# Attention units of one batch and four heads, with the second transposition moved from TensorE to the DMA queue of SyncE

## The chip, the cores and the metric

The kernel runs on one core of a Trainium2 chip. The metric is the device time of one execution in microseconds (us), as the median of several runs. A core has five engines with an instruction queue each: PE (TensorE: matmuls, which write to PSUM), DVE (VectorE), ACT (ScalarE), POOL (GpSimd) and SP (SyncE, which here only issues DMAs). Each engine works through its own queue strictly in order. [...]

## The reference

For 8 batches, 8 heads, 576 positions and a head size of 64, linear attention with a feature map of 128 + 128 features; then, on the eight heads side by side (512 features), a gated unit with a causal convolution of 5 taps:

```python
proj = q_or_k @ w_phi                              # 64 -> 128
proj = proj - max(abs(proj))                       # per position
phi = concat([exp(proj), exp(-proj)])              # 256 features
kv, z = phi(k).T @ v, sum(phi(k))                  # per head
x = (phi(q) @ kv) / (phi(q) @ z + 1e-6)
x = heads side by side                             # (8, 576, 512)
gate = sigmoid(sum over 5 taps of conv_w[tap] * x[position - 4 + tap])
out = (gate * (x @ w_val)) @ w_out
```

## The kernel before, in words

**Units and steps.** The attention is cut into 16 units. A unit of the kernel before is a pair of batches and a pair of heads (four units make a pair of batches); its Q, K and V are loaded for two units at a time by POOL, which casts them to bf16 on the way, into tiles of 128 partitions by 2 heads by 9 columns of 64 features. Two batches lie in the two partition halves of Q (`q_load`), while K and V are laid in four pieces (`kv_load`), so that eight of the nine columns hold one batch in all 128 partitions. Every unit takes three steps (`NG`), and `step(t)` writes the instructions of step t for all stages at once: K and Q of unit t // 3, the feature-major second projection three steps later (`LAGC`), the division seven steps later (`LAGN`). 48 steps carry units; the last steps only drain.

**The stages of a step**, by the letters of `ORDER`, which is the order in which their instructions enter the queues:

- K, k, x: PE projects K (`PK`), DVE takes the largest magnitude (`MK`), ACT writes the two exponentials (`KTIL`).
- T, t: PE transposes the K and Q of the next step (`T`), DVE copies them out (`QKT`).
- Q, q: PE projects Q (`PA`), DVE takes its maxima (`MQ`).
- C, c: PE projects Q once more in feature-major form (`PQ`), ACT writes the exponentials (`QTIL`).
- V, v (every third step): PE sums phi(k).T v (`KV`), DVE copies it (`KVSB`). V was scaled before on POOL (`VT`, two instructions of a unit).
- N, n: PE forms numerator and denominator (`NUM`), DVE divides (`RCP`, `XN`).
- X (three steps of twelve): PE transposes XN to feature-major form (`XP`), DVE copies that to `XT`, and POOL copies two shifted stretches of it for the taps (`emit_virt`).
- L, a, d: a list `mlp` of items of the gated unit. Each step adds `BUDGET[g]` to a purse and takes items as long as the purse is positive. An item is `emit_VG` (taps `GATE`, and `VAL`, on PE; then tanh `GS` on ACT and the product `GV` on DVE) or `emit_O` (output matmuls `OP`, copied by ACT to `OS`, stored by two DMAs of SP). What is left in the list after the last step is written behind it.

**PSUM.** `PK`, `PA`, `PQ`, `KV` and `GATE` take turns in three buffers of two banks, `T`, `NUM`, `XP`, `VAL` and `OP` in two buffers of one bank.

**A pair of batches as an amount of work for the gated unit:** four items with taps of 512 columns and two VAL results of 4 matmuls each, one small item (columns of chunk 8), and nine `OP`. They enter the list when both batches have all heads transposed: for the first pair at step 20, and for the last one behind step 55.

```python
BLOCKS = [[(ALL, b, c)] for b in range(2) for c in (0, 4, 1, 5)]
ORDER = "KkTtNVxQLnaCvXqdc"
LAGC, LAGV, LAGN, LAGM = 3, 4, 7, 1
BUDGET = (30, 30, 5)
```

## Time and profile before

| | |
|---|---|
| median of 3 runs | 270.02 us (269.23 to 270.37) |
| the profiled execution | 271.08 us |
| its span, first to last instruction | 269.3 us |
| PE busy | 227.3 us, 84% of the span |
| DVE busy | 192.3 us, 71% |
| ACT busy | 184.2 us, 68% |
| POOL busy | 142.3 us, 53% |
| mean granted TensorE clock | 0.949 of full speed |

A row of a timeline gives the start in us, the length in us, the engine, line, operation, output and inputs, and the number of instructions merged; in brackets stands how long the engine sat idle before and for whom it waited. Matmuls are pipelined, so the length of one overlaps the next; what a group costs PE is the distance from its start to the start of the next group. Shares over the whole span mix stages with different limits.

### The profile page before, as it was taken

The page shows a single profiled execution, that of the slowest core. Times are in us where ns is not written, and L with a number is a line of the kernel's source. Part 1 is how long each engine was busy: PE and PEld are TensorE (multiplying, and loading weights), DVE is VectorE, ACT ScalarE, POOL GpSimd, SP SyncE. Part 2 cuts the span into 40 slices and gives each one's busy share as a digit, 9 for nine tenths or more (in the row PEclk, how much of TensorE's full clock was granted, in tenths as well). Part 3 has the DMA queues.
Part 4 walks back from the last instruction along what each step waited for, and adds up shares of the span by engine and source line. Part 5 has one row for each costly group of instructions (what it writes and reads, how often), then busy time and mean ns, then how long its engine had stood idle before and what let it go on. Part 6 is the DMA issues. An engine that isn't in the chain of part 4 may idle for free.

```text
span 269.3 us, 8205 instructions
## 1 busy us (share of the span) xinstructions
PE 227.3 (84%) x3508; PEld 144.2 (54%) x3528; DVE 192.3 (71%) x342; ACT 184.2 (68%) x285; POOL 142.3 (53%) x190
## 2 busy tenths in 40 slices
PE   8578876676799988998799979987899899779992
PEld 4345665564656464666546455665555456533441
DVE  2597799999888497779878587888978553634221
ACT  1479799899576886988657777987569767111551
POOL 8979989999923945098416942336306060030000
PEclk9755799999999999999999999999999999977999
DMA  5999998925920894449800992520001505300536
GB/s 162 151 182 172 151 176 119 178 33 64 174 30 2 137 218 69 104 78 162 124 2 22 152 225 32 115 64 19 0 4 41 117 4 121 80 0 0 121 86 146
DMA packets 28948, 25.83 MB, mean 96 GB/s; under 512 B 2667, under 2 KB 24043, under 8 KB 28912
## 3 DMA queue, kind: packets, MB, share of 16 engines
q0 software_dynamic: 22128, 14.63, 39.5%
q1 hardware_dynamic: 6272, 10.06, 15.4%
q10 hardware_dynamic: 512, 0.62, 0.8%
q8 instruction: 27, 0.44, 0.7%
q14 instruction: 9, 0.07, 0.1%
HBM read 30.48 MB, written 9.44 MB: 148 GB/s over the span
## 4 chain that ended last, share of the span: by engine, by line
PE 48%; DVE 27%; ACT 18%; issue 3%; DMA 2%; ACTq 1%; POOL 0%; POOLq 0%; DVEq 0%
PE OP L471 12%; DVE MK L291 9%; PE VAL L463 9%; PE GATE L442 9%; ACT KTIL L296 9%; ACT QTIL L341 6%; DVE MQ L306 5%; DVE QKT L277 4%; PE KV L354 3%; PE NUM L376 3%; DVE XN L387 3%; PE XP L406 2%; PE PQ L329 2%; DVE GV L452 2%; ACT GS L448 2%
## 5 line engine op out<-in xcount | busy, mean ns | idle before, releaser
L317 POOL TENSOR_TENSOR VT<-VN,E 128x1152 bf16<-128x1152 bf16 x32 | 68.5, 2141 | 70.4 <-issue 61.7
L341 ACT ACTIVATE QTIL<-PQ 128x768 bf16<-128x768 f32 x96 | 73.2, 826 | 17.7 <-PE PQ L334 17.7
L296 ACT ACTIVATE KTIL<-PK 128x768 bf16<-128x768 f32 x96 | 73.1, 822 | 16.6 <-DVE MK L291 16.4
L452 DVE SCALAR_TENSOR_TENSOR GV<-GS,VAL 128x512 bf16<-128x512 bf16 (+1 forms) x40 | 24.8, 634 | 40.3 <-ACT GS L448 33.9
L291 DVE TENSOR_REDUCE MK<-PK 128x6 f32<-128x768 f32 x48 | 45.9, 956 | 9.6 <-PE PK L283 9.1
L306 DVE TENSOR_REDUCE MQ<-PA 128x6 bf16<-128x768 f32 x48 | 45.7, 951 | 0.0
L471 PE MATMUL OP<-WOUT,GV 128*128 128x512 bf16 x124 | 33.8, 379 | 4.9 <-DVE QKT L277 3.3
L448 ACT ACTIVATE GS<-GATE 128x1024 bf16<-128x1024 f32 (+1 forms) x20 | 18.8, 940 | 26.4 <-PE GATE L442 26.0
L463 PE MATMUL VAL<-XT,WVAL 128*128 128x512 bf16 (+1 forms) x192 | 36.4, 337 | 0.0
L476 ACT ACTIVATE OS<-OP 128x512 f32<-128x512 f32 x36 | 21.8, 607 | 13.3 <-PE OP L471 11.2
L376 PE MATMUL NUM<-KVSB,QTIL 128*128 128x65 bf16 (+1 forms) x640 | 29.9, 196 | 0.5 <-DVE XT L416 0.3
L283 PEld LDWEIGHTS <-QKT 64*128 64x128 bf16 x576 | 19.9, 98 | 18.6 <-issue 12.5
L277 DVE COPY QKT<-T 128x768 bf16<-128x768 bf16 (+2 forms) x49 | 27.6, 563 | 2.6 <-PE T L264 2.2
L387 DVE TENSOR_TENSOR XN<-NUM,RCP 128x384 bf16<-128x384 f32 x48 | 26.8, 558 | 1.6
L283 PE MATMUL PK<-W,QKT 64*128 64x128 bf16 x288 | 17.4, 229 | 12.1 <-ACT KTIL L296 9.6
L442 PE MATMUL GATE<-XT,DIAG 64*64 64x512 bf16 (+1 forms) x480 | 24.7, 338 | 2.0 <-POOL XT L423 1.2
L376 PEld LDWEIGHTS <-QTIL 128*128 128x128 bf16 (+1 forms) x640 | 24.6, 100 | 3.2 <-issue 0.7
L463 PEld LDWEIGHTS <-WVAL 128*128 128x128 bf16 x192 | 15.1, 100 | 19.6 <-issue 8.6
L264 PE MATMUL T<-ident_bf,QN 128*128 128x128 bf16 x144 | 23.3, 233 | 1.5 <-ACT QN L152 1.5
L264 PE MATMUL T<-ident_bf,KN 128*128 128x128 bf16 x144 | 23.7, 235 | 0.2 <-DVE KN L154 0.2
L471 PEld LDWEIGHTS <-GV 128*128 128x128 bf16 x144 | 13.0, 97 | 18.8 <-issue 4.0
L423 POOL COPY XT<-XT 128x504 bf16<-128x504 bf16 x16 | 9.3, 618 | 23.8 <-DVE XT L416 23.8
(50 smaller groups left out, 309.1 us busy)
## 6 DMA issues: line engine op xcount, KB each, us to landing
out_dram<-OS SPq DMA_DIRECT2D x72, 128.0 KB, 2.4
QN<-in_q_dram POOLq DMA_DIRECT2D x14, 288.0 KB, 7.5
VN<-in_v_dram POOLq DMA_DIRECT2D x16, 160.0 KB, 8.2
KN<-in_k_dram POOLq DMA_DIRECT2D x14, 160.0 KB, 5.3
VN<-in_v_dram POOLq DMA_DIRECT2D x16, 128.0 KB, 8.1
KN<-in_k_dram POOLq DMA_DIRECT2D x14, 128.0 KB, 4.4
WNAT<-in_moe_w_val_dram POOLq DMA_DIRECT2D x1, 512.0 KB, 7.5
WOUT<-in_moe_w_out_dram POOLq DMA_DIRECT2D x4, 128.0 KB, 7.2
```

Of the source, the lines that this page charges most:

```text
L264: nc.tensor.transpose(T[:, s * GC + i, :], src.rearrange("p h c d -> p (h c d)")[:, m * P:(m + 1) * P], ident_bf[:, :])
L277: nc.vector.tensor_copy(QKT[:, xs, :], T[:, xs, :])
L283: nc.tensor.matmul(PA[:, r, i * P:(i + 1) * P], u.T[g][half(r), s, i, :], W2[half(r), :], start=True, stop=True)
L291: nc.vector.tensor_reduce(u.MK[:, :].rearrange("p (m r) -> p r m", r=2)[:, :, blocks(g)], u.PK, AX.X, ALU.max, apply_absolute_value=True)
L296: nc.scalar.activation(u.KTIL[:, sg].rearrange("p (m r) f -> p r m f", r=2)[:, :, blocks(g), :], u.PK, AF.Exp, scale=1.0 - 2.0 * sg)
L306: nc.vector.tensor_reduce(mq, u.PA, AX.X, ALU.max, apply_absolute_value=True, negate=True)
L317: nc.gpsimd.tensor_tensor(VT[:, :, 0:D], u.VN.rearrange("p h c d -> p (h c) d"), eb.to_broadcast([P, 2 * NC, D]), ALU.mult)
L341: nc.scalar.activation(u.QTIL[:, sg, :, :, g * GC * D:(g + 1) * GC * D], PQ[:, :, 0:GT].rearrange("p r (b x) -> p r b x", b=2), AF.Exp, sc ...
L376: nc.tensor.matmul(NUM[ps, i, h, :], u.QTIL[:, sg, r, b, m * D:m * D + ps.stop - ps.start], u.KVSB[:, b, 2 * h + sg, :], start=(sg == 0), ...
L442: nc.tensor.matmul(GATE[half(c), r, z * n:(z + 1) * n], DIAG[half(r), jt, tap, :], cols(jt, 4 - tap, half(r)), start=(tap == 0), stop=(tap ...
L463: nc.tensor.matmul(VL[:, z, :], WVAL[:, dt, v * P:(v + 1) * P], cols(dt, 0), start=(dt == 0), stop=(dt == 3))
L471: nc.tensor.matmul(OP[:, :], pr.GV[g][:, jt // 2, jt % 2, i * P:(i + 1) * P], WOUT[:, jt, :], start=(jt == 0), stop=(jt == 3))
```

## The change

A unit is now one batch and four heads: heads 2hp and 2hp + 1 in the lower partition half, heads 4 + 2hp and 5 + 2hp in the upper one. K and V are loaded as Q is, by two DMAs each, where K and V took four. Every column of KTIL now holds two heads, so `pe_KV` works on partition halves throughout: 72 matmuls of 64 rows, where there were 32 of 128 rows and 8 of 64. A batch is finished every six steps, where a pair was finished every twelve.

XN is transposed into XT by DMA transposes that SP issues right behind the division of a batch's second unit (`dma_x`), ten for each of the first seven batches: eight of 128 positions by 256 features and two of 64 by 256. Only the last batch keeps the way by PE (`x_tile`), with one of its copies on ACT. POOL's shifted copies of a batch are written two steps behind its last transpose, and its items enter the list three steps behind it (`LAGX`).

The items of the gated unit are cut finer (taps, and each VAL result, apart) and are made per batch with 256 columns, the small item and its `OP` per pair. The budget is 8, 20 and 20 over the three steps of a unit, with the purse set to 0 while the list is empty. The letters of `ORDER` are rearranged: MQ's projection goes ahead of NUM, the products and the transposes last. At the start, 12 matmuls on zeros stand where there were 20, ACT and not POOL builds `EB`, and three loads fewer lead K and Q in. POOL's late constants move from steps 12 and 13 to 9 and 10.

```diff
-BLOCKS = [[(ALL, b, c)] for b in range(2) for c in (0, 4, 1, 5)]
+
+BLOCKS = [[(ALL, s, c)] for s, c in ((0, 0), (0, 4), (1, 0), (1, 4), (1, 1), (1, 5), (0, 1), (0, 5))]
 BLOCKS.insert(4, [(LO, 0, 8), (HI, 1, 8)])
+NB = len(BLOCKS)
...
-ORDER = "KkTtNVxQLnaCvXqdc"
+ORDER = "KTVkQtNxvnLCqadcX"
 LAGC, LAGV, LAGN, LAGM = 3, 4, 7, 1
-XACT = ()
-BUDGET = (30, 30, 5)
+LAGX = 3
+XACT = (8,)
+BUDGET = (8, 20, 20)
...
+    def load(T, x, u, nh, engs):
+        for s in range(2):
+            h0 = 4 * s + 2 * u.hp
+            engs[s % len(engs)].dma_start(T[half(s), 0:nh, :, :],
+                                          x[u.b, h0:h0 + nh].rearrange("h (p c) d -> p h c d", c=NC))
...
-    for i in range(20):
+    for i in range(12):
...
-        for c in range(4):
+        for c in range(NC):
             for n in range(4):
-                for b in range(2):
-                    cc = n // 2 * NC + c + 5 * b
-                    nc.tensor.matmul(kvv[:, b, n, :], u.KTIL[:, n % 2, cc, :], u.VT[n % 2][:, cc, :],
-                                     start=(c == 0 and n == 0), stop=False, skip_group_check=True)
-        for n in range(4):
-            for b in range(2):
-                cc = n // 2 * NC + 4
-                nc.tensor.matmul(kvv[:, b, n, :], u.KTIL[half(b), n % 2, cc, :], u.VT[n % 2][half(b), cc, :],
-                                 start=False, stop=True, skip_group_check=True)
+                for s in range(2):
+                    cc = n // 2 * NC + c
+                    nc.tensor.matmul(kvv[:, s, n, :], u.KTIL[half(s), n % 2, cc, :], u.VT[n % 2][half(s), cc, :],
+                                     start=(c == 0 and n == 0), stop=(c == NC - 1), skip_group_check=True)
...
+    def dma_x(bt, g):
+
+        for e in range(g * GC, g * GC + GC):
+            for rows, s, c in BLOCKS[e]:
+                nc.sync.dma_start_transpose(bt.XT[:, 2 * s:2 * s + 2, xcol(c):xcol(c) + rows.stop - rows.start],
+                                            bt.XN[rows, e].rearrange("p h d -> p (h d)"))
...
+        yield (12 if g < 2 else 9), gate
+        for r in range(2):
+            yield (9 if g < 2 else 6), lambda r=r: val(r)
...
+    def mlp_items(bt):
+
+        for g in range(2):
+            yield from gv_items([bt], g)
+        for g in range(2):
+            for i in range(2):
+                yield 9, lambda g=g, i=i: flush() or emit_O([bt], g, i)
+        if bt.b % 2 == 1:
+            two = batches[bt.b - 1:bt.b + 1]
+            yield from gv_items(two, 2)
+            yield 9, lambda: flush() or emit_O(two, 2, 0)
...
-        if t == 12:
+        if t == 9:
             late_consts()
-        if t == 13:
+        if t == 10:
...
+                if ux.hp == NHP - 1 and ux.bt is not batches[-1]:
+                    dma_x(ux.bt, gx)
+                    if gx == 2:
+                        ready[t + LAGX] = ux.bt
...
+            elif o == "X" and uy and uy.hp == NHP - 1 and uy.bt is batches[-1]:
+                for c in ((), (0, 4, 8), (1, 5))[gy]:
+                    x_tile(uy.bt, c)
                 if gy == 2:
-                    emit_virt(uy.pair, 1)
-                    ready[t + LAGM] = uy.pair
+                    emit_virt(uy.bt)
+                    ready[t + LAGM] = uy.bt
             elif o == "L":
-                budget = min(budget + BUDGET[g], 45)
+                budget = min(budget + BUDGET[g] / ORDER.count("L"), 45) if mlp else 0
...
+        if t + 1 in ready and ready[t + 1] is not batches[-1]:
+            emit_virt(ready[t + 1])
```

**What moves on SP.** SP's queue held only the first loads and the output stores. Before, from the last of the first loads on (OS is the finished output):

```order
L124 DMA K_96<-in_k_dram 64x2x320
L124 DMA K_96<-in_k_dram 64x2x256
L130 DMA Q_97<-in_q_dram 64x2x576
L481 DMA out_dram<-OS 64x512 [waits DMAHW0_49,Activation_49]
L481 DMA out_dram<-OS 64x512 [waits DMAHW1_49]
L481 DMA out_dram<-OS 64x512 [waits DMAHW2_49,Activation_49]
```

Now, from the last transposes of the second batch on to the first of the third (XT_151 and XT_152 are the two buffers of XT, DVE is the division):

```order
L405 DMA_TRANSPOSE XT_151<-XN 128x2x128 [waits DMAHW0_49]
L405 DMA_TRANSPOSE XT_151<-XN 128x2x128 [waits DMAHW1_49]
L478 DMA out_dram<-OS 64x512 [waits DMAHW2_49,Activation_49]
L478 DMA out_dram<-OS 64x512 [waits DMAHW3_49]
L478 DMA out_dram<-OS 64x512 [waits DMAHW4_49,Activation_49]
L478 DMA out_dram<-OS 64x512 [waits DMAHW5_49]
L478 DMA out_dram<-OS 64x512 [waits DMAHW6_49,Activation_49]
L478 DMA out_dram<-OS 64x512 [waits DMAHW7_49]
L478 DMA out_dram<-OS 64x512 [waits DMAHW0_49,Activation_49]
L478 DMA out_dram<-OS 64x512 [waits DMAHW1_49]
L405 DMA_TRANSPOSE XT_152<-XN 128x2x128 [waits DMAHW2_49,DVE_49]
L405 DMA_TRANSPOSE XT_152<-XN 128x2x128 [waits DMAHW3_49]
```

Ten transposes of a batch now stand in one queue with the stores, each behind the one that was issued eight DMAs earlier (DMAHW0 to DMAHW7), and no store passes a transpose that waits.

**What moves on POOL.** Here stand the scaling of V for two units and the shifted copies between them. Before:

```order
L317 TENSOR_TENSOR VT_1368<-VN,E 128x18x64 [waits PE_49,Activation_49]
L319 CAST VT_1368<-E 128x18
L423 COPY XT_169<-XT_169 128x4x2x63 [waits DVE_49] x3
L423 COPY XT_169<-XT_169 128x4x2x63
L317 TENSOR_TENSOR VT_1702<-VN,E 128x18x64 [waits PE_49,Activation_49,Pool_49]
L319 CAST VT_1702<-E 128x18
L317 TENSOR_TENSOR VT_1705<-VN,E 128x18x64 [waits PE_49,Activation_49,Pool_49]
L319 CAST VT_1705<-E 128x18
```

Now, at the first batch:

```order
L306 TENSOR_TENSOR VT_936<-VN,E 128x18x64 [waits PE_49,Activation_49]
L308 CAST VT_936<-E 128x18
L413 COPY XT_151<-XT_151 128x4x2x63 [waits DMAHW7_49,DMAHW5_49]
L413 COPY XT_151<-XT_151 128x4x2x63 [waits DMAHW3_49,DMAHW2_49,DMAHW1_49]
L306 TENSOR_TENSOR VT_1193<-VN,E 128x18x64 [waits PE_49,Activation_49]
L308 CAST VT_1193<-E 128x18
L306 TENSOR_TENSOR VT_1196<-VN,E 128x18x64 [waits PE_49,Activation_49]
L308 CAST VT_1196<-E 128x18
```

The shifted copies waited for DVE and now wait for DMA transposes, and the next unit's scaling of V is queued behind them.

**What moves on DVE.** A step with transposition before (XT is the copy of the transposed heads), and one at the same stage now:

```order
L416 COPY XT_169<-XP 128x4x128 [waits PE_49] x3
L306 TENSOR_REDUCE MQ_109<-PA 128x2x3
L291 TENSOR_REDUCE MK<-PK 128x2x3 [waits PE_49,Activation_49]
L277 COPY QKT<-T 128x896 [waits PE_49]
L384 RECIPROCAL RCP<-NUM 128x6 [waits PE_49]
L387 TENSOR_TENSOR XN_523<-NUM,RCP 128x3x128 [waits DVE_49]
L366 CAST KVSB<-KV 128x520 [waits PE_49]
L416 COPY XT_169<-XP 128x4x128 [waits PE_49]
```

```order
L280 TENSOR_REDUCE MK<-PK 128x2x3 [waits PE_49,Activation_49]
L266 COPY QKT<-T 128x896 [waits PE_49]
L350 CAST KVSB<-KV 128x520 [waits PE_49]
L368 RECIPROCAL RCP<-NUM 128x6 [waits PE_49]
L370 TENSOR_TENSOR XN<-NUM,RCP 128x3x128 [waits DVE_49]
L295 TENSOR_REDUCE MQ_107<-PA 128x2x3
L280 TENSOR_REDUCE MK<-PK 128x2x3 [waits PE_49]
```

The copies to XT are gone from DVE; the copy of KV now goes ahead of the division.

## Rows read from the trace of the kernel before

**Rows 1.** The table by stage: busy us of each engine (instructions), clock, DMA.

```profile
17.60:56.50 38.90, 29.05 (x546) 22.90 (x545) 34.53 (x56) 35.20 (x56) 37.63 (x58) 0.84 1.10 156
...
76.80:135.40 58.60, 52.33 (x875) 34.03 (x880) 47.30 (x86) 44.93 (x70) 32.55 (x41) 1.00 0.61 103
...
239.00:269.30 30.30, 25.21 (x201) 10.18 (x203) 6.25 (x10) 10.08 (x14) 0.49 (x1) 0.89 0.34 78
```

**Rows 2.** Line 291 on DVE, once a step: count, min/median/max ns, first to last start.

```profile
L291 DVE TENSOR_REDUCE MK<-PK x16: 949/958/960, 11.0 to 56.5; 128x6 f32<-128x768 f32 x16
...
L291 DVE TENSOR_REDUCE MK<-PK x13: 949/958/961, 76.8 to 135.4; 128x6 f32<-128x768 f32 x13
...
L291 DVE TENSOR_REDUCE MK<-PK x4: 951/958/960, 193.9 to 212.7; 128x6 f32<-128x768 f32 x4
```

**Rows 3.** PE's timeline, steps 33 and 34, with KV, an output pair and a tap item.

```profile
142.75 0.55 PE L376 MATMUL NUM<-KVSB,QTIL 128*128 128x65 bf16 x12
143.13 1.14 PE L354 MATMUL KV<-VT,KTIL 128*128 128x65 bf16 x32
144.20 0.29 PE L359 MATMUL KV<-VT,KTIL 64*128 64x65 bf16 x8
144.33 0.33 PE L283 MATMUL PA<-W,QKT 64*128 64x128 bf16 x6
...
146.43 0.34 PE L329 MATMUL PQ<-QKT,W 64*128 64x384 bf16 x2
...
147.03 0.23 PE L264 MATMUL T<-ident_bf,KN 128*128 128x128 bf16 x1
...
147.38 0.54 PE L376 MATMUL NUM<-KVSB,QTIL 128*128 128x65 bf16 x12
147.85 0.34 PE L283 MATMUL PA<-W,QKT 64*128 64x128 bf16 x6
148.62 1.89 PE L471 MATMUL OP<-WOUT,GV 128*128 128x512 bf16 x7 [0.42 <-DVE QKT L277]
150.43 1.27 PE L442 MATMUL GATE<-XT,DIAG 64*64 64x512 bf16 x20
151.64 1.90 PE L463 MATMUL VAL<-XT,WVAL 128*128 128x512 bf16 x8
153.47 0.34 PE L329 MATMUL PQ<-QKT,W 64*128 64x384 bf16 x2
```

**Rows 4.** PE's timeline, a small item.

```profile
174.15 0.75 PE L442 MATMUL GATE<-XT,DIAG 64*64 64x128 bf16 x40
174.84 1.07 PE L463 MATMUL VAL<-XT,WVAL 128*128 128x128 bf16 x16
175.84 0.34 PE L329 MATMUL PQ<-QKT,W 64*128 64x384 bf16 x2
```

**Rows 5.** Groups by line and shape: busy us, mean ns, idle before and releaser.

```profile
L406 PE MATMUL XP<-ident_bf,XN 128*128 128x128 bf16 x144 | 12.7, 219 | 6.8 <-DVE QKT L277 2.5 <-DVE XN L387 2.4 <-DVE XT L416 1.9
...
L416 DVE COPY XT<-XP 128x512 bf16<-128x512 bf16 x32 | 12.8, 421 | 4.2 <-PE XP L406 3.5
```

**Rows 6.** The timeline of the end: the last pair's first items, the last copy.

```profile
238.99 2.47 PE L442 MATMUL GATE<-XT,DIAG 64*64 64x512 bf16 x20 [1.19 <-POOL XT L423]
241.39 3.60 PE L463 MATMUL VAL<-XT,WVAL 128*128 128x512 bf16 x8
...
264.91 0.60 ACT L476 ACTIVATE OS<-OP 128x512 f32<-128x512 f32 x1 [1.75 <-PE OP L471]
```

**Rows 7.** DMA issues and queues: KB each and us to landing; packets, MB, share.

```profile
q1 hardware_dynamic: 6272, 10.06, 15.4%
...
out_dram<-OS SPq DMA_DIRECT2D x72, 128.0 KB, 2.4
...
VN<-in_v_dram POOLq DMA_DIRECT2D x16, 160.0 KB, 8.2
```

**Rows 8.** Line 481, SP's stores: issue ns min/median/max, first and last start.

```profile
L481 SPq DMA_DIRECT2D out_dram<-OS x72: 466/593/2048, 87.7 to 266.0; - x72
```

## The prediction

> **What bounds the kernel now.** I start with the table by stage. While a pair's gated unit is being worked off, between 76.8 and 135.4 us, PE is busy for 52 of 58.6 us, DVE for 47 and ACT for 45; before that, between 17.6 and 56.5 us, no gated unit exists yet and DVE (34.5 of 38.9 us) and ACT (35.2) are the full ones [rows 1]. The reader is to see two regimes that take turns. Next come the step lengths, from the row of the line that runs once a step. Step 15 starts at 56.5 us, steps 20 to 32 take 58.6 us, that is 4.88 us each, and step 47 starts at 212.7 us [rows 2]; the attention-only steps 3 to 15 take 38.9 / 12 = 3.24 us [rows 1]. What PE needs for itself comes from its timeline, by the distance between starts: PQ and PK 0.60, T 0.35, PA 0.27, together 1.22 us in every step; NUM 0.47 for 12 matmuls, so 39 ns each, 40 in a unit; KV with its tail 1.20 in every third step [rows 3]. A unit of three steps is 3.66 + 0.06 + 1.56 + 1.20 = 6.5 us. Of the gated unit, taps of 512 columns take 1.21 for 20 matmuls, their VAL 1.83 for 8, an output tile 0.91 [rows 3], the small item 0.69 + 1.00 [rows 4]: a pair is 4 x 3.04 + 1.69 + 9 x 0.91 = 22.0 us. With 36 transposes at about 56 ns, the spacing of T [rows 3], twelve steps need 26.0 + 22.0 + 2.0 = 50 us of PE, and take 58.6. So 8.6 us of twelve steps are neither matmul nor weight: in steps with much of the list PE is the bound and the others wait, in steps with transposition or an empty list the DVE and ACT chain is.

> **The change, part by part, against the profiled span of 269.3 us.**

> *Transposes.* PE loses 7/8 of 144 transposes, some 2 us of a pair, and the 6.8 us it idled before them; DVE loses copies of 421 ns, 12.8 us in all for the large form [rows 5]. In place of them SP gets 70 DMAs (63 in units of 64 KB). No row shows a transposing DMA. From below, a store of 128 KB takes 0.59 us to issue [rows 8] and lands after 2.4 us [rows 7], so 0.6 us each in a row. From above, nearest is POOL's casting load, 8.2 us to landing [rows 7], if none overlapped. In between, SP's and ACT's DMAs cost 15.4% of 16 x 269.3 us over 6,272 packets, 106 ns per packet [rows 7]; if a transpose moves 256-byte pieces (one row of 128 features), 64 KB is 256 of them, 1.7 us over 16 engines. I take 1.7, since it is of the same kind of queue, and keep both ends. A batch then needs 9 x 1.7 = 15.3 us plus 2.4 for landing, from a step's middle on; five steps of 4 us lie between its first transpose and its first taps. It just fits: cost nothing, covered by those steps. If the cover goes, PE stands at GATE and POOL at the shifted copies, with the next scaling of V behind them.

> [...] On the TensorE side the trace decides: one transpose lasts 219 ns [rows 5] and the next follows 56 ns later [rows 3].

> *KV on halves.* 72 matmuls of 64 rows against 32 + 8. The eight of that form take 0.13 us here, 16 ns each, from 144.20 to 144.33 [rows 3]; 72 are 1.17 us against 1.20. Nothing. If pairs of halves did not overlap, they would cost what full ones do, 33 ns [rows 3], 2.4 us, 1.2 us more in each of 16 units; the row is of the very form, so I don't take it.

> *Finer items of 256 columns.* Twice the instructions at half the columns. 512 columns are 60 ns a tap [rows 3], 128 are 17 ns [rows 4]; the line between gives 31 ns, 1.23 us for 40. VAL: 229 and 62 ns give 118, 0.94 for 8. Same work within 0.1 us an item. ACT's and DVE's pieces keep their sizes.

> *Loads.* POOL issues 48 loads where there were 80; POOL bounds nothing in rows 1 after the start. Q is issued one DMA earlier, 0.6 us [rows 8]. ACT's building of EB and 8 warm-up matmuls fewer lie under the wait for Q: 0. I take 0.5 us.

> *The new order of steps.* The list now begins at step 15 and gets 16 points of budget a step, where an OP of 0.91 us costs 9. By the order of PE's instructions, steps 15 to 46 hold 10 tap items, 20 VAL results, 2 small items and 19 output tiles: 12.1 + 18.4 + 3.4 + 17.3 = 51.2 us, at most 2.2 us in a step. The attention of these 32 steps is 10.67 x 6.5 = 69.3 us. Every step then holds more PE work (3.3 us and up) than the 3.24 us of the DVE and ACT chain, so PE is the bound throughout. To that come PE's waits: step 33, with KV, has none (its pieces add up to the 4.63 us from NUM to NUM), step 34 has 0.50 us after PA, from 148.12 to 148.62, most of it on QKT [rows 3]; two such steps in three make 0.33 us. So 69.3 + 51.2 + 32 x 0.33 = 131 us. From step 15 (56.5 - 0.5 = 56.0) step 47 starts at 187.0, where it was 212.7.

> *The end.* From step 47 PE has left 6 tap items, 12 VAL, 2 small items and 17 output tiles, 37.2 us, which is more than before, since the budget falls behind; 9.5 us of attention and transposes; 9 x 0.33 of waits and 0.5 in the last small item. The last copy and store take 269.3 - 264.9 = 4.4 us [rows 6]. Less 0.3, since the row marks a step 0.3 us after its PK: 37.2 + 9.5 + 3.0 + 0.5 + 4.4 - 0.3 = 54.3 us, against 56.6 before. [...]

> *Sum.* 187.0 + 54.3 = 241.3 us of span. The profiled execution took 1.8 us more than its span and 1.1 us more than the median, so the median would be 242, 28 us below 270.0. Of the 28, some 6 are transposes taken off PE by step 47, 6 are items put off, 14 are PE's idling in unbalanced steps, 2 the end and the start.

> **The rivals.**

> 1. *Forecast:* 242 us; its own range 236 to 249 (waits of 0.15 to 0.5 us a step).
> [...]
> 3. *Even steps couple worse.* PE has 3.8 us of work a step, ACT 44.9 / 12 = 3.7 and DVE (47.3 - 4) / 12 = 3.6 [rows 1]: no engine has slack. At the PE share of steps 20 to 32, 50 / 58.6 = 0.85, the 120.5 us become 141, 10 us more: 252. Against: step 33 ran without a gap.
> 4. *Slower: the transpose queue becomes the bound.* 63 units of x us start at 42 us; behind the last one stand two batches of items and the end, 27 us. That is 269.3 at x = 3.2. Beyond it the kernel is slower: at 4 us, 42 + 252 + 27 + 1 = 322. For it: nothing shows x, and the casting load's 8.2 us is above it. Against: the packet price, 1.7.
> 5. *Nothing gained*, x near 3.2: 270.

> **How the numbers follow.** Forecast 0.5, late transposes 0.2, coupling 0.17, slower 0.11, nothing 0.02. Predicted is the forecast, 242 us. The range holds rivals 2 and 3 with some margin and leaves out rival 4: 233 (no waits at all, 32 x 0.33 less) to 261. About 0.5% is what a measurement of this kernel tells from no change. Faster 0.87, same 0.02, slower 0.11.

> **What would show it.** Line 280, once a step, should run from step 15 to 47 in 131 us, 4.1 us a step with little spread. KV should stay near 1.2 us on PE. DMA transposes should land within 3 us of issue, ten of them within 18 us; POOL's copies (line 413) and GATE should wait for none after the first batch. The last stretch should hold the full clock. Wrong I am if step 47 starts after 200 us, if the waits of PE name DMA, or if SP is issuing without a break.

## The result, and the profile after

The changed kernel takes 262.11 us (median of 4 runs, 260.11 to 265.01) against 269.62 for the kernel before in the same job: a ratio of 0.970 (0.963 to 0.976). It is faster by 3%, where 10% was forecast; the time lies one microsecond above the range. The profiled execution took 262.3 us with a span of 260.4. The ratios, here and below, leave out single executions that were more than 1.5% slower than the fastest of their kernel, such as the one of 265.01 us.

The profile page of the changed kernel, parts 1, 3 and 6 (DMA queues: packets, MB, share of the 16 engines' time; q0 has POOL's loads, q8 the instructions):

```profile
PE 220.6 (85%) x4354; PEld 156.2 (60%) x4354; DVE 180.9 (69%) x306; ACT 186.9 (72%) x288; POOL 120.8 (46%) x156
...
q0 software_dynamic: 13680, 14.63, 36.6%
q1 hardware_dynamic: 24496, 14.20, 31.3%
...
q8 instruction: 34, 0.56, 0.9%
...
out_dram<-OS SPq DMA_DIRECT2D x72, 128.0 KB, 2.4
...
XT<-XN SPq DMA_TRANSPOSE x70, 5.7
```

The queue of SP's and ACT's DMAs carries 24,496 packets where it carried 6,272 [rows 7]: the transposes are what was added to it. The row on instructions looks like nothing. It becomes the main one below: 4354 matmuls and 4354 weight loads are 8708 instructions, and 8708 / 34 packets (0.56 MB in all) is 256 instructions for each packet of 16 KB.

The table by stage (columns as in [rows 1]), for a stretch of full lists, the one after it, and the end:

```profile
82.60:139.80 57.20, 50.17 (x1070) 36.01 (x1069) 44.07 (x73) 44.07 (x69) 27.66 (x32) 0.97 0.81 128
139.80:204.40 64.60, 58.82 (x1279) 42.56 (x1278) 54.20 (x93) 54.08 (x86) 29.72 (x32) 1.00 0.50 86
204.40:260.40 56.00, 48.34 (x825) 32.49 (x824) 20.59 (x42) 26.37 (x40) 6.85 (x8) 0.98 0.42 96
```

In the first of these stretches PE is busy for 88%, hardly less than the 89% of [rows 1]; in the second, with fewer loads, for 91%. The line that runs once a step, DVE's line 280 from step 15 to 47 (as [rows 2]), and SP's line 405, the transposes (issue ns):

```profile
L280 DVE TENSOR_REDUCE MK<-PK x33: 948/953/962, 59.6 to 204.4; 128x6 f32<-128x768 f32 x33
```

```profile
L405 SPq DMA_TRANSPOSE XT<-XN x70: 1165/1244/2346, 43.6 to 219.9; - x70
...
DMA to landing us min/median/max: 2.3/5.7/11.1
```

Step 15 starts at 59.6 us (56.0 forecast), step 47 at 204.4 (187.0), and the end takes 56.0 (54.3). The spread of the steps tells more than their sum. Most take 4.0 to 4.4 us, as forecast, but 18, 24, 30 and 36 take 6.2, 7.0, 6.9 and 6.6, and 12 takes 5.7: every sixth. The waits of PE, in all and then on its timeline around step 24 and in the other four (in brackets the idle time before the row, and what ended it):

```profile
PE NUM L360 <- issue: 7.7, 4, 2.3
...
PE KV L343 <- issue: 1.7, 1, 1.7
...
PE GATE L435 <- POOL XT L413: 0.3, 1, 0.3
```

```profile
100.33 1.27 PE L343 MATMUL KV<-VT,KTIL 64*128 64x65 bf16 x72
101.44 0.33 PE L272 MATMUL PA<-W,QKT 64*128 64x128 bf16 x6
101.70 0.46 PE L360 MATMUL NUM<-KVSB,QTIL 128*128 128x65 bf16 x9
103.94 0.26 PE L360 MATMUL NUM<-KVSB,QTIL 128*128 128x65 bf16 x3 [1.79 <-issue]
...
50.56 0.30 PE L343 MATMUL KV<-VT,KTIL 64*128 64x65 bf16 x8 [1.65 <-issue]
...
76.15 0.26 PE L360 MATMUL NUM<-KVSB,QTIL 128*128 128x65 bf16 x3 [1.56 <-issue]
...
133.23 0.36 PE L360 MATMUL NUM<-KVSB,QTIL 128*128 128x65 bf16 x6 [2.28 <-issue]
...
160.30 0.35 PE L360 MATMUL NUM<-KVSB,QTIL 128*128 128x65 bf16 x6 [2.05 <-issue]
```

KV itself takes 1.11 us (100.33 to 101.44). Then PE stands in the middle of a row of twelve equal matmuls, after nine, with nothing that it waits for: "issue". No tile is late, no other engine is named, and PE hardly waits for the transposes. Counting the instructions of PE ahead of the first one behind each pause (the 36 of its sequencer, which wait for semaphores, counted too), and reading the times of the packets on the instruction queue, gives this table:

```
step  instructions ahead of it      packet begins, ends  PE resumes
12    1217                          47.84   49.08        50.56
18    2241                          73.29   74.68        76.15
24    3265                          101.23  102.51       103.94
30    4289                          130.67  131.73       133.23
36    5313                          157.86  158.82       160.30
```

The five places are exactly 1024 = 4 x 256 instructions apart, and each time PE goes on 1.43 to 1.50 us after a packet of 256 instructions has landed. So the theory: PE stands because its next block of instructions is not there. Six steps, two units, hold nearly four blocks, so a border meets every second KV burst at the same place: in it or right behind it. The burst is 72 matmuls with their weight loads, 144 instructions in 1.11 us; nowhere does PE go through instructions faster. PE had needed only some 4.4 us from the preceding border to each of the last four pauses, and 6.4 to the first; the packets in question began 3.2 to 5.4 us after that preceding border.

### The profile page after: what moved, and what is told of

Same layout as the page of the kernel before. It is cut to its first block, busy times and chain, and to the rows that moved or that the text cites. A ratio compares the mean times of both kernels' runs of the same rounds, so it can differ in the third digit from the quotient of the medians.

```text
span 260.4 us, 9923 instructions
## 1 busy us (share of the span) xinstructions
PE 220.6 (85%) x4354; PEld 156.2 (60%) x4354; DVE 180.9 (69%) x306; ACT 186.9 (72%) x288; POOL 120.8 (46%) x156
## 3 DMA queue, kind: packets, MB, share of 16 engines
q1 hardware_dynamic: 24496, 14.20, 31.3%
## 4 chain that ended last, share of the span: by engine, by line
PE 48%; DVE 24%; ACT 16%; issue 7%; DMA 3%; ACTq 1%; POOL 0%; POOLq 0%
PE OP L468 11%; DVE MK L280 8%; PE VAL L449 8%; PE GATE L435 7%; ACT KTIL L285 6%; PE KV L343 6%; DVE MQ L295 5%; ACT QTIL L330 4%; PE NUM L360 4%; DVE QKT L266 4%; PE T L253 3%; DVE GV L454 3%; ACT GS L441 3%; DMA Q<-in_q_dram 3%; PE PQ L318 2%
## 5 line engine op out<-in xcount | busy, mean ns | idle before, releaser
L306 POOL TENSOR_TENSOR VT<-VN,E 128x1152 bf16<-128x1152 bf16 x32 | 67.8, 2119 | 56.3 <-issue 30.4
L449 PE MATMUL VAL<-XT,WVAL 128*128 128x256 bf16 (+1 forms) x320 | 37.5, 266 | 2.7 <-DVE QKT L266 2.3
L360 PE MATMUL NUM<-KVSB,QTIL 128*128 128x65 bf16 (+1 forms) x640 | 31.3, 197 | 8.4 <-issue 7.7
L468 PE MATMUL OP<-WOUT,GV 128*128 128x512 bf16 x144 | 35.3, 379 | 2.9 <-DVE QKT L266 1.6
L360 PEld LDWEIGHTS <-QTIL 128*128 128x128 bf16 (+1 forms) x640 | 23.8, 101 | 16.0 <-issue 8.8
L413 POOL COPY XT<-XT 128x504 bf16<-128x504 bf16 x16 | 9.3, 607 | 52.0 <-DMA XT<-XN 46.4
L449 PEld LDWEIGHTS <-WVAL 128*128 128x128 bf16 x320 | 27.5, 99 | 8.9 <-issue 5.7
L272 PEld LDWEIGHTS <-QKT 64*128 64x128 bf16 x576 | 20.7, 100 | 16.2 <-issue 8.6
L441 ACT ACTIVATE GS<-GATE 128x1024 bf16<-128x1024 f32 (+1 forms) x20 | 18.8, 941 | 12.1 <-PE GATE L435 11.9
L253 PE MATMUL T<-ident_bf,QN 128*128 128x128 bf16 x144 | 24.4, 240 | 2.4 <-ACT QN L141 2.4
L253 PE MATMUL T<-ident_bf,KN 128*128 128x128 bf16 x144 | 24.6, 241 | 1.7 <-DVE KN L143 1.7
L435 PE MATMUL GATE<-XT,DIAG 64*64 64x256 bf16 (+1 forms) x800 | 23.6, 261 | 2.5 <-ACT KTIL L285 1.5
L272 PE MATMUL PK<-W,QKT 64*128 64x128 bf16 x288 | 17.7, 234 | 8.0 <-ACT KTIL L285 5.0
L468 PEld LDWEIGHTS <-GV 128*128 128x128 bf16 x144 | 13.2, 97 | 17.3 <-issue 3.5
## 6 DMA issues: line engine op xcount, KB each, us to landing
VN<-in_v_dram POOLq DMA_DIRECT2D x16, 288.0 KB, 10.8
```

The lines of the kernel that those rows point to most:

```text
L253: nc.tensor.transpose(T[:, s * GC + i, :], src.rearrange("p h c d -> p (h c d)")[:, m * P:(m + 1) * P], ident_bf[:, :])
L272: nc.tensor.matmul(PA[:, r, i * P:(i + 1) * P], u.T[g][half(r), s, i, :], W2[half(r), :], start=True, stop=True)
L306: nc.gpsimd.tensor_tensor(VT[:, :, 0:D], u.VN.rearrange("p h c d -> p (h c) d"), eb.to_broadcast([P, 2 * NC, D]), ALU.mult)
L360: nc.tensor.matmul(NUM[ps, i, h, :], u.QTIL[:, sg, r, b, m * D:m * D + ps.stop - ps.start], u.KVSB[:, b, 2 * h + sg, :], start=(sg == 0), ...
L435: nc.tensor.matmul(GATE[half(c), r, w * n:(w + 1) * n], DIAG[half(r), jt, tap, :], cols(jt, 4 - tap, half(r)), start=(tap == 0), stop=(tap ...
L449: nc.tensor.matmul(VL[:, w, :], WVAL[:, dt, v * P:(v + 1) * P], cols(dt, 0), start=(dt == 0), stop=(dt == 3))
```

## The experiments

**1. Move the borders.** 72 matmuls of two columns, into the scratch bank of the warm-up, move every later instruction of PE by 144 places, and change nothing else. The theory is called A in the expectations; beside it stand the rivals that each of them names.

```
+    for i in range(72):
+        nc.tensor.matmul(wps[:, 0:2], MQbs[0], MQ3[:, 0, 0:2], start=True, stop=True)
```

> The changed kernel with 72 tiny matmuls (2 columns) behind the 12 warm-up ones, and nothing else; they fill idle PE time before Q arrives. Theory A (instruction blocks): PE stands 1.7 to 2.5 us in five steps because its next block of 256 instructions has not arrived; the 144 instructions more move the block borders away from the end of the 72 KV matmuls. Then the pauses in the NUM of steps 18, 24, 30 and 36 (6.2 to 7.0 us long) vanish, these steps fall to some 4.5 us, smaller pauses may show elsewhere, and the time is 252 to 257 us, ratio to the kernel before 0.935 to 0.955. Rival B (late transposes hold POOL's shifted copies, so V is scaled late and KV waits): the same steps stay at 6 to 7 us, 262 us.

Measured: 253.98 us (253.62 to 255.49), ratio 0.945 (0.938 to 0.951), span 252.1. More work, and 8 us less. The same waits, and the stage behind step 16:

```profile
PE GATE L437 <- issue: 1.2, 2, 0.7
PE KV L345 <- issue: 0.5, 1, 0.5
```

```profile
64.50:196.90 132.40, 122.20 (x2647) 89.37 (x2657) 112.64 (x189) 112.87 (x176) 68.21 (x78) 1.00 0.77 115
```

Steps 18, 24, 30 and 36 take 4.4 us each, 17.7 together where they took 26.7.

**2. Move the borders by a whole block.** 128 such matmuls are 256 instructions, so the borders fall where they fell in the changed kernel. If the gain of experiment 1 came from something else at the start, such as more warm-up, it should stay.

```
-    for i in range(72):
+    for i in range(128):
```

> As the shift by 72 tiny matmuls, but with 128, that is 256 instructions, so that the borders of the instruction blocks fall on the same instructions of the steps as in the changed kernel itself. Theory A (block borders): the pauses of about 2 us in NUM of steps 18, 24, 30 and 36 come back, and the time is 259 to 263 us although more tiny matmuls run. Rival C (the tiny matmuls help by keeping PE active, and its clock up, ahead of the first step): as with 72, 252 to 256 us, and no pauses.

Measured: 261.42 us (260.72 to 261.88), ratio 0.972 (0.968 to 0.975). The pauses are back, in the same steps and at the same matmuls:

```profile
PE NUM L362 <- issue: 6.7, 4, 2.1
PE KV L345 <- issue: 1.9, 1, 1.9
```

The two runs differ by 56 tiny matmuls and by 7.4 us. The mean granted clock was 0.985 in the profiled execution here and 0.936 in that of the changed kernel, at nearly the same time, so the clock is not the cause.

**3. Move the loads.** Why is the packet late? POOL's casting loads are in flight at most of these places. Here they leave three steps earlier, and PE's instructions stay as they are.

```
-            if i % 2 == 0 and i // 2 + 2 < NU // 2:
-                load_two(i // 2 + 2)
+            if i == 0:
+                load_two(2)
+            if i % 2 == 1 and i // 2 + 3 < NU // 2:
+                load_two(i // 2 + 3)
```

> The changed kernel with the loads of two units issued three steps earlier, behind the scaling of V of odd units, so that they fly before the transposes and not beside them. Theory A1 (block fetches start 3 to 5 us late because loads and transposes are in flight together): fetches beside transposes start within 2 us, the pauses of steps 18 to 36 fall below 1 us, 253 to 257 us. Theory A2 (the transposes alone delay the fetches): pauses as before, 260 to 263 us.

Measured: 259.87 us (257.43 to 264.07), ratio 0.962 (0.954 to 0.970). Steps 18, 24, 30 and 36 take 4.4 us with their borders unmoved. But step 27 now takes 7.2, with a pause at GATE, and step 12 keeps its own:

```profile
PE GATE L435 <- issue: 2.7, 2, 2.1
PE KV L343 <- issue: 1.4, 1, 1.4
```

So a border was not enough here: the pauses came where PE was fast (4.4 to 6.4 us from the border before, in the changed kernel) and the packet came while loads were in flight. The mechanism held, the size did not: the early loads made new pauses, and step 15 longer (5.9 us).

The packets of the changed kernel itself say the same. Thirteen times POOL's loads were in flight between PE's passing of a border and the beginning of the next packet, and that took 2.1 to 5.4 us. The other 21 packets began at most 0.9 us after the border, among them two beside transposes but no loads (185 and 192 us).

**4. Both.** Experiments 1 and 3 together.

> Both edits of the first two runs together. Theory A: whichever of the two does more is approached, 250 to 256 us, with no pause over 1 us left. Rival B: 260 us or more.

Measured: 257.7 us (255.36 to 258.08), ratio 0.955 (0.949 to 0.962): a miss. Step 15 took 9.6 us, since the first batch's transposes came late beside the early loads:

```profile
PE GATE L437 <- POOL XT L415: 5.3, 4, 3.5
```

**5. No transposing DMAs.** All batches are transposed by PE, as the last one is. The edit, in the loop over a step's operations:

```
-                if ux.hp == NHP - 1 and ux.bt is not batches[-1]:
-                    dma_x(ux.bt, gx)
-                    if gx == 2:
-                        ready[t + LAGX] = ux.bt
-            elif o == "X" and uy and uy.hp == NHP - 1 and uy.bt is batches[-1]:
+            elif o == "X" and uy and uy.hp == NHP - 1:
...
-        if t + 1 in ready and ready[t + 1] is not batches[-1]:
-            emit_virt(ready[t + 1])
```

> The changed kernel with all batches, not the last alone, transposed on PE and copied by DVE and ACT; no DMA transposes. The block borders move as well, since PE gets 36 instructions more per batch. If DMA transposes are what makes fetches late (A2): no pause of over 1 us within a block, and 255 to 262 us, the gain from the missing pauses set against 7 x 2 us of PE and the DVE copies. If the loads alone delay them (A1 or simpler): fetches still start 3 us late in the steps behind loads, pauses at some border, 264 to 270 us.

Measured: 262.14 us (261.8 to 262.81), ratio 0.974 (0.969 to 0.979), span 260.1. The time is that of the changed kernel, for another reason: pauses of PE on "issue" were few (the longest 0.9 us), but PE and DVE were longer at work, and steps 30, 36 and 42, which hold the transposes, took 6.0 to 6.6 us.

```profile
PE 227.2 (87%) x4459; PEld 161.2 (62%) x4480; DVE 190.4 (73%) x334; ACT 190.1 (73%) x295; POOL 120.9 (46%) x156
```

By its time and its pauses the run fits A2 as it was written, so the packets have to decide: beside loads they still began 2.1 to 4.5 us after PE had passed the preceding border, with no transposing DMA in the kernel. The loads alone delay them; the forecast time of that case, 264 us and more, did not come. The place of the borders changes with the transposes too, so what the DMAs are worth is read against experiment 1, where PE's pauses are small as well: 262.1 against 254.0, some 8 us.

**6. One step more for the transposes.** In experiment 1 POOL's shifted copies still wait for the transposes for 48.3 us in all. Here the copies and the list's items come one step later, on top of experiment 1.

```
-LAGX = 3
+LAGX = 4
```

> The shift by 72 tiny matmuls, and LAGX 4 in place of 3: a batch's items enter the list, and its shifted copies are queued on POOL, one step later. If late transposes of the first batch cost what step 15 shows (6.3 us where 4.1 was forecast): step 15 falls to 3.5 us and the time by 1 to 2 us, to 252 to 253. If PE is busy enough that a wait only moves the work into the end: 254 to 256 us, since one more step of items is left for the end.

Measured: 269.54 us (268.24 to 270.31), ratio 1.000 (0.998 to 1.002): the whole gain is gone, and both expectations were wrong. POOL's timeline before the first batch's taps, and PE's later on:

```profile
61.70 2.12 POOL L308 TENSOR_TENSOR VT<-VN,E 128x1152 bf16<-128x1152 bf16 x1
63.76 0.27 POOL L310 CAST VT<-E 128x18 bf16<-128x18 f32 x1
63.89 1.28 POOL L121 DMA_DIRECT2D KN<-in_k_dram  x2
65.14 1.26 POOL L121 DMA_DIRECT2D QN<-in_q_dram  x2
66.34 1.28 POOL L121 DMA_DIRECT2D VN<-in_v_dram  x2
67.55 1.23 POOL L415 COPY XT<-XT 128x504 bf16<-128x504 bf16 x2
```

```profile
68.29 0.30 PE L437 MATMUL GATE<-XT,DIAG 64*64 64x256 bf16 x4 [3.34 <-POOL XT L415]
...
102.06 1.34 PE L437 MATMUL GATE<-XT,DIAG 64*64 64x256 bf16 x13 [5.50 <-POOL XT L415]
```

The copies no longer wait for transposes, but for one of 8.2 us near the end. They stand behind two scalings of V (the second is shown) and six load issues in POOL's queue, and PE stands for them: 9.7 us in all, 5.5 at once. Behind that wait PE also ran slower: its granted clock was 0.62 from 102 to 108 us, and the 40 taps took 2.6 us where they take 1.2 (the row of the first 13 above lasts 1.34 us; that of 36 in experiment 1 lasts 1.18). The mean granted clock of the profiled execution was 0.921 here and 0.981 in experiment 1. The same edit also moves which items meet which steps; the two were not told apart.

**7. EB on POOL again.** Step 0 starts at 11.7 us, 0.7 later than before. In the kernel before, POOL built EB ahead of its first loads. On top of experiment 1:

```
-        nc.scalar.activation(EB[rows, :, :],
-                             ident_bf[rows, r * D:r * D + NC].unsqueeze(2).to_broadcast([D, NC, P]), AF.Copy)
+        nc.gpsimd.tensor_copy(EB[rows, :, :],
+                              ident_bf[rows, r * D:r * D + NC].unsqueeze(2).to_broadcast([D, NC, P]))
```

> The kernel of the first experiment (72 tiny matmuls at the start), with EB built on POOL again, so that POOL's first loads leave 2.3 us later, as they did in the kernel before. Theory (POOL's earlier loads compete with Q's first load): POOL's first load starts near 5.3 us in place of 3.0, Q's first cast near 8.8 us in place of 9.2, step 0 near 11.0 to 11.2 us in place of 11.7, and the span is 0.3 to 0.7 us shorter than the first experiment's 252.1 if nothing else gets late. Rival (Q comes late for other reasons, its two halves in queues of two engines): Q's first cast stays at 9.2 us, and the span stays or grows, since V and the second unit's K come later.

Measured: 253.72 us (253.55 to 254.35), ratio 0.941 (0.938 to 0.945); no difference from experiment 1. Q's first cast starts at 8.79 us as in the kernel before, and step 0 at 11.3. But step 15 takes 8.2 us in place of 6.3:

```profile
59.36 0.43 PE L345 MATMUL KV<-VT,KTIL 64*128 64x65 bf16 x17 [0.84 <-issue]
...
61.88 0.30 PE L437 MATMUL GATE<-XT,DIAG 64*64 64x256 bf16 x4 [1.43 <-POOL XT L415]
62.43 1.85 PE L437 MATMUL GATE<-XT,DIAG 64*64 64x256 bf16 x36 [0.25 <-POOL XT L415]
```

These waits are only 0.7 us longer than in experiment 1; but from 62.0 to 65.4 us the granted clock was 0.61 here and 1.00 there, and the 36 taps took 1.85 us here and 1.18 there.

The start is not settled: in the eight profiles with POOL's early loads Q's cast came anywhere between 8.9 us (the next experiment) and 10.0 (experiment 3).

**8. The first batch transposed by PE.** On top of experiment 1; the edit is that of experiment 5 for the first batch alone.

```
-                if ux.hp == NHP - 1 and ux.bt is not batches[-1]:
+                if ux.hp == NHP - 1 and ux.bt not in (batches[0], batches[-1]):
...
-            elif o == "X" and uy and uy.hp == NHP - 1 and uy.bt is batches[-1]:
+            elif o == "X" and uy and uy.hp == NHP - 1 and uy.bt in (batches[0], batches[-1]):
...
-        if t + 1 in ready and ready[t + 1] is not batches[-1]:
+        if t + 1 in ready and ready[t + 1] not in (batches[0], batches[-1]):
```

> The kernel of the first experiment, with the first batch transposed by TensorE, as the last one is (its nine units are not sent through SP's transposing DMAs; 63 - 9 whole units and their small ones remain). Theory (step 15 was 6.3 us long since the first batch's transposing DMAs came late beside the loads): step 15 is 4.0 to 5 us long, no wait of POOL for a DMA of XT before it, and the time falls by 1 to 2 us, to 252 to 253, less what the transposes and their copies add to steps 12 to 15 on TensorE and DVE, some 1 us. Rival (the length of step 15 is that of a full list beginning, whoever transposes): step 15 stays at 6 us and the time at 254 or above.

Measured: 254.59 us (252.95 to 255.89), ratio 0.943 (0.937 to 0.949). Step 15 takes 4.4 us, so the late transposes were what made it long; but steps 12 to 14 take 13.2 us in place of 10.3, and step 16 starts at 64.7 where it started at 64.6. PE's transposes cost what the wait had cost. Nor did the time fall to the 252 to 253 us expected. One pause at a block border came back, in step 25:

```profile
103.58 0.70 PE L362 MATMUL NUM<-KVSB,QTIL 128*128 128x65 bf16 x10 [1.81 <-issue]
```

The best versions are experiments 1 and 7, at 0.945 and 0.941 of the kernel before, with intervals that overlap. Over all ten traces the places agree: each of the 22 pauses of PE on "issue" that are longer than 0.5 us stands at a border of the same count, within the few records that some traces lack.

## Why the prediction was wrong, point by point

The span came out at 260.4 us in place of 241.3. Experiment 1 splits these 19.1 us: 8.3 go with the place of the block borders (260.4 - 252.1), 10.8 stay.

*The step that failed first: finer items ("Same work within 0.1 us an item") and KV on halves ("Nothing").* The columns were priced, and rightly: 72 KV matmuls take 1.11 us (1.17 forecast). The instructions were not. The edit brings PE from 3528 weight loads to 4354, with a matmul to each, and packs 144 of them into 1.1 us. Where loads were in flight, blocks of 256 were used up faster than they came: of 27 blocks before, none ended in such a pause, of the 34 after, five did. Before, packets began up to 3.6 us after a border too, but PE took 7.4 us or more for each block beside them, where it now took 4.4 ahead of four of the five pauses. Which of the two finer cuts weighs more was not tested: no run undoes one alone. No rival held this, since all of them took PE's waits to be waits for an engine or a DMA of the program. In the kernel before, PE, the packets of instructions, and all that PE stood on "issue":

```profile
PE 227.3 (84%) x3508; PEld 144.2 (54%) x3528; DVE 192.3 (71%) x342; ACT 184.2 (68%) x285; POOL 142.3 (53%) x190
...
q8 instruction: 27, 0.44, 0.7%
```

```profile
PE OP L471 <- issue: 0.2, 1, 0.2
```

*PE's work was sized too small, by 5.5 us.* The forecast put 116.7 us of matmuls into the 31 steps from 16 on (120.5 / 32 a step) and 0.33 us of waits a step. In experiment 1 PE is busy for 122.2 of these 132.4 us. The rest, 10.2, is 0.33 a step: the sum of the waits came out, by some luck, since 1.2 of it are pauses on "issue" that the forecast did not hold; the work did not. The warning stood in [rows 1]: the sum of spacings made 50 us of a stretch in which the table had PE busy for 52.33, and 122.2 / 116.7 is the same 1.047. One cause is the new order of groups. A step of experiment 1, from the first transpose T to the group behind it:

```profile
76.61 0.23 PE L255 MATMUL T<-ident_bf,KN 128*128 128x128 bf16 x1
...
76.91 0.22 PE L255 MATMUL T<-ident_bf,QN 128*128 128x128 bf16 x1
77.06 0.34 PE L274 MATMUL PA<-W,QKT 64*128 64x128 bf16 x6
```

From its start to the next group T costs 0.45 us here, where it was priced at 0.35 from a row in which NUM follows it [rows 3]. Now PA or KV follows, 0.15 us after the last transpose and not 0.06. That is 0.1 us in each of the 31 steps, by estimate some 3 of the 5.5; so the equal factor is in part chance. Rival 3 foresaw a loss of this kind, of 10 us, at the PE share of the stretch before, by waits among the engines; but PE's idle time did not grow. Since the ends of matmuls are modelled in that table, whether the rest of the 5.5 us is slower work or short waits inside a group was not told apart.

*The transposes: the mechanism right, the price off, the cover mostly there.* SP issues one in 1.24 us and ten in a row in 14.8 to 15.9; 1.7 each and 18 us for ten had been the figures. But they land after 5.7 us in the median, and up to 11.1, where 3 was said. POOL's copies stood 46.4 us for them, which was to happen once at most, and yet PE lost 0.3: the cover reached over it. In experiment 1, where PE is quicker to get there, the cover of the first batch falls short:

```profile
61.52 1.16 POOL L415 COPY XT<-XT 128x504 bf16<-128x504 bf16 x2 [4.93 <-DMA XT<-XN]
62.64 2.12 POOL L308 TENSOR_TENSOR VT<-VN,E 128x1152 bf16<-128x1152 bf16 x1
```

```profile
62.18 0.30 PE L437 MATMUL GATE<-XT,DIAG 64*64 64x256 bf16 x4 [1.09 <-POOL XT L415]
62.73 1.18 PE L437 MATMUL GATE<-XT,DIAG 64*64 64x256 bf16 x36 [0.25 <-POOL XT L415]
```

This is, in small, the case of late transposes, to which the prediction gave 0.2: step 15 takes 6.35 us in place of 4.1, 2.3 too many (PE's waits for the copies are 1.3 of them, and one on "issue" in KV is 0.5), and the next scaling of V stands behind the copies, as written. The time per transpose behind that case and its place in the range is shown by no run; what the trace shows is the 1.24 us to issue and the 5.7 to landing. Rivals 4 and 5 are refuted: the queue of transposes is no bound. The queue's start, put at 42 us in rival 4 (step 15 at 56.0, less five steps of 3.24, and half a step on), came at 43.6, and ten transposes took at most 15.9 us of the 27 in which six steps bring a batch (59.6 to 204.4 us is 32 steps).

*The start* was to gain 0.5 us and lost 0.7 at step 0; in experiment 1 step 15 starts at 58.2, 2.2 late. Experiments 7 and 8 change the start by 0.3 to 0.4 us but not the total, so this part stays open. *The end* was right: 56.0 us, 55.1 in experiment 1, against 54.3. The first items behind the last transposes ran at a granted clock of 1.00 (232.0 to 235.2 us), 40 taps of 256 columns in 1.29 us and 16 VAL in 1.92. In the kernel before, the same columns took 2.47 and 3.60 us [rows 6], at a granted clock of 0.50 (239.0 to 245.0 us):

```profile
232.02 1.29 PE L435 MATMUL GATE<-XT,DIAG 64*64 64x256 bf16 x40
233.24 1.92 PE L449 MATMUL VAL<-XT,WVAL 128*128 128x256 bf16 x16
```

The account of experiment 1 closes: 2.2 to step 15, 2.3 in it, 5.5 on to step 47, 0.8 in the end make 10.8. Of the signs named beforehand, "step 47 after 200 us" came true (204.4), while no wait of PE names a DMA and SP does not issue without a break: the slip was found by the step lengths, and its cause was not among those listed. The lower end of the range was mis-added: no waits at all are 242 - 10.6 = 231 us, not 233. That changes nothing here.

## What to carry to other kernels

Halving tiles doubles instructions: besides columns, count the matmuls and weight loads of TensorE, and where it stands on "issue" in the middle of a row of equal matmuls, look whether such places are a multiple of 256 instructions apart, as the five here were (1024). Here the loop's period, six steps, was close to a whole number of blocks, four, and 72 dummy matmuls before it were worth 3 per cent, from 262.1 to 254.0 us; where a loop looks like that, they are worth a try. And check a sum of spacings against the busy time of a known stretch before it carries a forecast, and take the spacing at the end of a group from a place where the same group follows it.
